# Attention into a channel mix: the first part's values in one PSUM tile, and a new order of all tasks

## The chip, the cores and the metric

The kernel runs on one core of one Trainium2 chip. The metric is the device time of one execution in microseconds, taken as the median of several. The profiles are single executions of the same program, recorded by the hardware profiler.

## The reference

Two stages for 8 batches of 576 positions. The first is attention in 8 heads of 64 channels with a mask that is causal by blocks of 64; the second takes its output as 512 channels and mixes them.

```python
scores = scale * np.matmul(q, k.transpose(0, 1, 3, 2))       # [8, 8, 576, 576]
scores = np.where(block_i >= block_j, scores, -1e9)          # blocks of 64
attn = np.exp(scores - max); attn = attn / (attn.sum(-1) + 1e-9)
x = np.matmul(attn, v)                                       # -> [8, 576, 512]
xk = mu_k * x + (1.0 - mu_k) * x_prev                        # x_prev: one position back
xr = mu_r * x + (1.0 - mu_r) * x_prev
k = np.maximum(xk @ w_k, 0.0)                                # 512 -> 1024
out = 1.0 / (1.0 + np.exp(-(xr @ w_r))) * (k * k @ w_v)      # 512 -> 512, 1024 -> 512
```

All inputs and the output are float32 in the chip's main memory.

## The kernel before

**Tasks.** The kernel is a list of 961 tasks, each for one engine: a load, a cast, a group of matmuls, an exponential and so on. They are written down in a fixed numbering. `ORDER` is a list of these numbers, written out by hand in the source, and gives the order in which they are issued; each engine works through its own tasks in that order. `PLACE` names for each flexible task (casts, squares, subtractions, copies out of PSUM) the engine that does it: P for GpSimd, D for VectorE, A for ScalarE. SyncE issues all transfers, also in the order of the list. A number with `+n` in `ORDER` puts n matmuls ahead of a TensorE task whose result nothing reads (`unread`, L253); they fill time in which TensorE would idle. A `B` task of the values does not issue its own, even where the list has a number for it.

**Buffers.** `RINGS` gives each kind of tile a number of buffers, and a task that needs a new one takes the one that was released first in the order of the list. PSUM has eight banks of 2 KB for each partition: three `s` tiles of two banks (`[128, 2, 512]` float32) and two `mm` tiles of one bank (`[128, 512]` float32). `s` tiles hold the transposed queries and keys, the scores, and the sums and values of the attention. `mm` tiles hold the products of the channel mix; at the start one of them is the target of the filling matmuls.

**A batch.** Queries and keys are loaded (`ld`), cast to bf16 (`nl`) and turned: in batches 0 to 2 by TensorE (`qt`, L312) with a copy out of PSUM (`ev`, L236 on ScalarE, L242 on VectorE), later by transposing transfers (`turn`, L357). Score tasks (`sc`, L458) write `s` tiles, ScalarE takes the exponential into `e` tiles (`ex`, L469). The values of attention are formed in two channel halves, A and B, by tasks `av`: A and B with the values (L517; L640 in batch 0), S with ones, which gives the sums (L507; L634). The sums are turned by VectorE (`t1`), inverted (`rec`), spread (`t2`), and `norm` multiplies them into the values and writes `x` (`xt`).

**Parts.** Batch 0 is done in two parts, positions 0 to 255 and 256 to 575, by `add_av_part` (`part` 0 and 1), so that the channel mix can begin early; the other batches are done in one by `add_av`. In the order A, S, B, the first task takes the even blocks of both halves and the last the odd ones. Task B starts with a scrap matmul into an unused corner of the sums' tile (L650), which makes TensorE wait until `t1` (L667) has read the sums.

**Before, each part takes three `s` tiles:**

```python
m = {kind: plan.buf("s") for kind in "SAB"}
```

one for the sums, of which one bank is used, and one for each channel half, with 256 or 320 columns in either bank. `norm` (L691) reads the half's tile and releases it.

**The channel mix.** For each batch and group of 128 channels there is a subtraction (`d`, L707) and a `mul` for `xk` and for `xr` (L729). Rows are then taken in chunks of 512 over the batches: `pk` multiplies with `WK` (L776), `relu` and `sq` give the squares in `k2` (L787, L789, L796, L798), `pr` multiplies with `WR` (L811), `tanh` follows (L821), `pv` multiplies with `WV` (L842), and `o` joins both (L854). `store` writes two tiles of 128 rows (L867). The weights are loaded as `ld` tiles and cast (`w`).

Of the kernel before, what the change touches and what calls it, by code (L numbers as in the profile page):

```python
# [14 lines left out]
LONGS = 3  # L15

ORDER = """
# [50 lines left out]
"""  # L68

PLACE = (  # L70
    "PPDPADPDPDDPPPAAPAAAADAADDDDDPPPPDPPPPDADDDPDDDPAPPPPDDAAPDDPAPAPA"
    "DDDPDDPDAAPDDDDAPAPDPPDDPAPAPDDPDPDPDDPPDPPDPAPDADDDAAPAADPDADPDDA"
    "PDAAPDDDADADAAADDAPAAAAAPAADPAAAPAADPDAAPAAADAPDPAPDAAADADAAPAPAPA"
    "AAAAADPAADAADADAAAPDPAAAAAPAPADAPADAPAPADAPAPAAAPADAPADDD")


class Plan:
# [53 lines left out]
def kernel(  # L131
# [12 lines left out]
    nc = tc.nc  # L144
    B, H, S, D = q.shape
# [44 lines left out]
    def new(buf):  # L190

        return slots[buf["ring"], buf["slot"]]
# [294 lines left out]

    HALVES = {"A": [*range(0, JT, 2)], "B": [*range(1, JT, 2)]}
    HALF = S // 2

    def blocks(b, PA, kind, ts=None):

# [120 lines left out]
    def add_av_part(b, part):  # L613
# [8 lines left out]
        exps = [ready["x", b, pr, i] for pr, i in its]  # L622
        vals = [cast["v", b, g] for g in range(2)] + [cast["vt"]]
        ebufs = [tiles["ebuf", b, it] for it in its]
        m = {kind: plan.buf("s") for kind in "SAB"}
        av = {}

        def products(f, t, at, n, i, col):
            for c in range(GH):
                E = new(tiles["ebuf", b, (c // 2, i)])  # L630
                out = slice(c * QC, (c + 1) * QC)
                flags = dict(start=t == 0, stop=t == pieces[-1][0])
                if f == "S":
                    nc.tensor.matmul(new(m[f])[out, 0, at:at + n],  # L634
                                     pick[:, (c ^ t) & 1],
                                     E[:, (c ^ t) & 1, col:col + n], **flags)
                    continue
                for u in range(2):
                    rows, w = weight(b, u, c, t, f)
                    nc.tensor.matmul(new(m[f])[out, u, at:at + n], w,  # L640
                                     E[rows, (c ^ t) & 1, col:col + n], **flags)

        tt, rc, rt = plan.buf("d"), plan.buf("rc"), plan.buf("rt")
        for kind in "ASB":
            def fn(eng, me, kind=kind):
                if kind != "B":
                    unread(me, new(m[kind])[:, 0])
                else:

                    nc.tensor.matmul(  # L650
                        new(m["S"])[0:QC, 0, CH - QC:CH], pick[:, 0],
                        new(ebufs[0])[:, 0, 0:QC], start=True, stop=True)
                for f in {"S": "S", "A": "AB", "B": "BA"}[kind]:
                    for t, lo, i, col, n in pieces:
                        if kind == "S" or t in HALVES[kind]:
                            products(f, t, lo, n, i, col)
            deps = exps + (vals if kind != "S" else [])
            if kind != "A":
                deps.append(t1m if kind == "B" else av["A"])
            av[kind] = add(  # L660
                f"av {b} {part} {kind}", "PE", fn, deps,
                uses=([m["S"]] if kind != "A" else [])
                + ([m["A"], m["B"], vo_buf[b]] if kind != "S" else [])
                + ebufs)
            if kind == "S":
                def t1(eng, me):
                    nc.vector.transpose(new(tt)[:, 0:W],  # L667
                                        new(m["S"])[:, 0, 0:W])
                t1m = add(f"t1 {b} {part}", "DVE", t1, [av["S"]],
                          uses=[tt, m["S"]])  # L670

        NB = W // QC

# [13 lines left out]
        for f in range(2):  # L687
            def norm(eng, me, f=f):
                x = new(xtbuf[b])[:, :, 1 + q_lo:1 + q_hi].rearrange(
                    "p (u f) t -> p u f t", f=2)  # L690
                nc.vector.tensor_tensor(  # L691
                    x[:, :, f], new(m["AB"[f]])[:, :, 0:W],
                    new(rt)[:, :, 0:W], ALU.mult)
            evac.setdefault(("x", b, part, f), []).append(
                add(f"norm {b} {part}{'AB'[f]}", "DVE", norm,
                    [av["B"]] + t2s, uses=[m["AB"[f]], rt, xtbuf[b]]))

    mixed = {}
    HC = CH // 2

    def add_mix(b, cc, part):
        d = plan.buf("d")
# [251 lines left out]
```

## Time and profile before

| | |
|---|---|
| median of 3 runs | 258.71 us (258.39 to 260.61) |
| the profiled execution | 258.73 us, its span 256.9 us |
| matmuls | 3425, TensorE busy 242.9 us |
| VectorE, ScalarE, GpSimd busy | 179.5, 172.8 and 83.8 us |
| mean granted TensorE clock | 0.992 |
| loaded and stored | 33.69 MB read, 9.44 MB written |

The span goes from the first to the last instruction on any engine. A busy share is taken over all of it. The granted clock is the share of full speed that TensorE was given. A row of the timeline has a start and a duration, the engine, the line of the kernel, the operation, the tile written and the tiles read, the shapes and the count; brackets behind it give the engine's idle time ahead of it and what ended that. A row of the groups has the busy time and the mean of one instruction in ns. "issue" as a releaser means that the engine waited for nothing that the profile shows.

### The profile page before, as it was taken

To read this page: it belongs to the slowest core of one execution; us is meant where nothing else is said; L and a number is where in the kernel's file an instruction comes from. 1 tells how busy PE (TensorE), PEld (TensorE's weight loads), DVE (VectorE), ACT (ScalarE), POOL (GpSimd) and SP (SyncE) were. 2 spreads that over 40 slices of the span, in tenths; PEclk is the share of its full clock that TensorE was granted. 3 is DMA by queue.
4 is the path that set the end of the run, shared out by engine and by line. 5 is a ranking of instruction groups with operands and counts; after the bars stand their busy time and mean duration, and the time that the engine had idled before them with its cause. 6 is when DMAs were issued, how large, how long until landed. Compare 5 with 4: busy or idle time off the path is not lost.

```text
span 256.9 us, 7885 instructions
## 1 busy us (share of the span) xinstructions
PE 242.9 (95%) x3425; PEld 121.8 (47%) x3425; DVE 179.5 (70%) x267; ACT 172.8 (67%) x234; POOL 83.8 (33%) x81
## 2 busy tenths in 40 slices
PE   7787779989999989999999999999999999999994
PEld 2454455745454435444544454445443554444452
DVE  1475969769879686997386978769868388622532
ACT  3597559989968866789688937974786851462330
POOL 2441356461334303302631026313613225170600
PEclk9999799999999999999999999999999999999999
DMA  7997999999999999999999999999961200400404
GB/s 215 393 282 172 391 287 243 348 258 176 270 207 160 261 206 199 233 229 232 198 192 268 185 171 208 276 234 214 194 149 74 92 3 0 164 4 0 165 3 163
DMA packets 119987, 49.54 MB, mean 193 GB/s; under 512 B 109584, under 2 KB 109840, under 8 KB 119952
## 3 DMA queue, kind: packets, MB, share of 16 engines
q1 hardware_dynamic: 119952, 49.04, 84.4%
q8 instruction: 27, 0.44, 0.8%
q14 instruction: 8, 0.07, 0.1%
HBM read 33.69 MB, written 9.44 MB: 168 GB/s over the span
## 4 chain that ended last, share of the span: by engine, by line
PE 79%; DVE 7%; DMA 5%; ACT 3%; issue 3%; SPq 2%; DVEq 0%; ACTq 0%
PE t_mm L776 24%; PE t_mm L842 21%; PE t_mm L811 11%; PE t_s L458 7%; PE t_s L517 7%; PE t_s L507 4%; DMA out_dram<-t_o 3%; SPq L225 2%; DMA t_ld<-in_q_dram 2%; DVE t_xk L729 2%; PE t_mm L253 2%; ACT t_e L469 1%; PE t_s L640 1%; ACT t_qkt L236 1%; DVE t_xt L691 1%
## 5 line engine op out<-in xcount | busy, mean ns | idle before, releaser
L469 ACT ACTIVATE t_e<-t_s 128x1024 f16<-128x1024 f32 (+3 forms) x98 | 87.8, 957 | 16.9 <-PE t_s L458 16.6
L776 PE MATMUL t_mm<-t_xk,WK 128*128 128x512 f16 (+1 forms) x320 | 69.7, 358 | 1.3 <-DVE t_xk L729 0.8
L842 PE MATMUL t_mm<-WV,t_k 128*128 128x512 f16 (+1 forms) x296 | 66.4, 374 | 0.3 <-DVE t_o L854 0.3
L798 POOL TENSOR_TENSOR t_k<-t_kr 128x512 f16<-128x512 f32 x30 | 34.0, 1141 | 73.2 <-ACT t_kr L787 43.0
L776 PEld LDWEIGHTS <-WK 128*128 128x128 f16 x320 | 29.3, 97 | 33.0 <-issue 7.6
L787 ACT ACTIVATE t_kr<-t_mm 128x512 f32<-128x512 f32 x48 | 28.7, 598 | 23.6 <-PE t_mm L776 23.5
L842 PEld LDWEIGHTS <-t_k 128*128 128x128 f16 x296 | 28.1, 98 | 33.8 <-issue 2.9
L854 DVE SCALAR_TENSOR_TENSOR t_o<-t_t,t_mm 128x512 f32<-128x512 f32 (+1 forms) x37 | 24.8, 670 | 24.6 <-PE t_mm L842 15.9
L811 PE MATMUL t_mm<-WR,t_xr 128*128 128x512 f16 x144 | 35.8, 380 | 0.0
L821 ACT ACTIVATE t_t<-t_mm 128x512 f32<-128x512 f32 x36 | 21.4, 597 | 16.8 <-PE t_mm L811 16.7
L458 PE MATMUL t_s<-t_qkt 64*64 64x64 bf16 (+7 forms) x680 | 29.1, 284 | 2.3 <-DVE t_xt L691 1.3
L729 DVE SCALAR_TENSOR_TENSOR t_xk<-t_d,MUK,t_xt 128x576 f16<-128x576 f32 (+4 forms) x44 | 29.7, 706 | 0.7 <-POOL t_d L707 0.6
L729 DVE SCALAR_TENSOR_TENSOR t_xr<-t_d,MUR,t_xt 128x576 f16<-128x576 f32 (+4 forms) x44 | 29.1, 671 | 1.1 <-POOL t_d L707 1.0
L707 POOL TENSOR_TENSOR t_d<-t_xt 128x576 f32<-128x576 f32 (+1 forms) x15 | 17.7, 1188 | 22.1 <-DVE t_xt L602 10.0
L458 PEld LDWEIGHTS <-t_qkt 64*64 64x64 bf16 x680 | 14.5, 106 | 20.4 <-issue 16.5
L242 POOL CAST t_nl<-t_ld 128x1152 bf16<-128x1152 f32 (+1 forms) x17 | 17.4, 1035 | 20.6 <-DMA t_ld<-in_k_dram 15.5
L789 DVE TENSOR_SCALAR t_kr<-t_mm 128x512 f32<-128x512 f32 x24 | 16.3, 684 | 8.7 <-PE t_mm L776 8.6
L796 ACT ACTIVATE t_k<-t_kr 128x512 f16<-128x512 f32 x29 | 17.9, 631 | 5.9 <-PE t_mm L842 5.3
L517 PE MATMUL t_s<-t_e,t_vo 64*32 64x64 f16 (+7 forms) x1106 | 20.6, 285 | 0.9 <-issue 0.9
L811 PEld LDWEIGHTS <-t_xr 128*128 128x128 f16 x144 | 12.9, 97 | 16.0 <-issue 2.5
L242 POOL CAST t_vo<-t_ld 128x1152 f16<-128x1152 f32 x9 | 10.2, 1145 | 31.4 <-DMA t_ld<-in_v_dram 31.4
L517 PEld LDWEIGHTS <-t_vo 64*32 64x32 f16 x1106 | 14.1, 92 | 10.4 <-issue 6.7
(51 smaller groups left out, 186.0 us busy)
## 6 DMA issues: line engine op xcount, KB each, us to landing
t_ld<-in_v_dram SPq DMA_DIRECT2D x32, 288.0 KB, 5.3
out_dram<-t_o SPq DMA_DIRECT2D x17, 512.0 KB, 4.1
t_ld<-in_q_dram SPq DMA_DIRECT2D x24, 288.0 KB, 5.3
t_ld<-in_k_dram SPq DMA_DIRECT2D x24, 288.0 KB, 5.2
t_ld<-in_k_dram SPq DMA_DIRECT2D x4, 576.0 KB, 7.8
t_ld<-in_q_dram SPq DMA_DIRECT2D x4, 576.0 KB, 8.1
t_ld<-in_moe_w_k_dram SPq DMA_DIRECT2D x4, 512.0 KB, 7.6
t_ld<-in_moe_w_v_dram SPq DMA_DIRECT2D x4, 512.0 KB, 6.6
```

Source lines behind the costliest of these rows:

```text
L242: e.tensor_copy(dst, src)
L458: nc.tensor.matmul(PS[y * D:y * D + D, x, col:col + n], operand(b, u, c, 1)[:, t * D:t * D + D], operand(b, u, c, 0)[:, q0:q0 + n], start= ...
L469: nc.scalar.activation(new(ebuf)[:, :, 0:w], new(m)[:, :, 0:w], AF.Exp, scale=ISQ)
L517: nc.tensor.matmul(PA[out, u, HALF + f * D:HALF + f * D + D] if kind == "T" else PA[out, u, lo - D:lo - D + n], w, E[rows, bank, at:at + n ...
L729: nc.vector.scalar_tensor_tensor(around[name][:, cc, at:at + w], new(d)[:, lo:lo + w], (MUK1, MUR1)[n][:, cc:cc + 1], x, ALU.mult, ALU.add)
L776: nc.tensor.matmul(ps[:, n], WK[:, cc, jc * P:(jc + 1) * P], xk[:, cc, lo:lo + w], start=(cc == 0), stop=(cc == CCn - 1))
L787: nc.scalar.activation(new(kr), new(m), AF.Relu)
L798: (nc.vector if eng == "DVE" else nc.gpsimd).tensor_tensor(dst, KR, KR, ALU.mult)
L811: nc.tensor.matmul(new(m), xr[:, cc, jt * P:(jt + 1) * P], WR[:, cc], start=(cc == 0), stop=(cc == CCn - 1))
L821: nc.scalar.activation(new(tb), new(m), AF.Tanh, scale=0.5)
L842: nc.tensor.matmul(new(m)[:, 0:w], k2[:, jc, jt * P:(jt + 1) * P], WV[:, jc, lo:lo + w], start=(jc == 0), stop=(jc == JCn - 1))
L854: nc.vector.scalar_tensor_tensor(new(o)[:, u, lo:lo + w], new(tiles["tbf", c, jt])[:, lo:lo + w], 1.0, new(m)[:, 0:w], ALU.add, ALU.mult)
```

## The change

`add_av_part` asks whether both halves of the part fit side by side: a part of up to 256 positions (`HC`) gets one `s` tile for A and B, B behind A in either bank, and its sums go to an `mm` tile. Only the first part of batch 0 is so short. Since A and B then share banks, only matmuls of A carry the start and stop flags. The second part, of 320 positions, keeps three `s` tiles. Besides, `ORDER` and `PLACE` are new throughout: all tasks are in another order, with other filling matmuls, and flexible tasks move between engines.

```diff
 ORDER = """
-11 12 15 0+12 17 18 13 14 16 51 52 49 50 73+3 3 74 127 128 7 5 125 75 9 6 79
-121 69+4 80 70 4 123 139+1 19 126 21 8 76 10 71 72 140 45 46 124 77+2 23 47
...
+11 12 17 0+12 13 14 49+1 15 16 18 50 7 8 51 9 10 3 5 125 52 121 47+4 6 71 48
+72 19 67 21 68 79+5 126 77 78 4 80 45+1 75 137 46 23 53+1 122 76 59 138 54
...
 PLACE = (
-    "PPDPADPDPDDPPPAAPAAAADAADDDDDPPPPDPPPPDADDDPDDDPAPPPPDDAAPDDPAPAPA"
...
+    "PPDDADDPDDDDAAAPAAADADDAADDPDDPPPPPDDDPDADADPPDDPPPPPDADAPDDDDPDPD"
...
 def add_av_part(b, part):
...
-        m = {kind: plan.buf("s") for kind in "SAB"}
+        one = W <= HC
+        ab = [plan.buf("s") for _ in range(1 if one else 2)]
+        sums = plan.buf("mm" if one else "s")
         av = {}
+
+        def dest(f):
+            if f == "S":
+                return new(sums) if one else new(sums)[:, 0]
+            n = "AB".index(f)
+            if one:
+                return new(ab[0])[:, :, n * W:(n + 1) * W]
+            return new(ab[n])[:, :, 0:W]
...
-                flags = dict(start=t == 0, stop=t == pieces[-1][0])
+                mine = f in "SA" or not one
+                flags = dict(start=mine and t == 0,
+                             stop=mine and t == pieces[-1][0])
...
-                    nc.tensor.matmul(new(m[f])[out, u, at:at + n], w,
+                    nc.tensor.matmul(dest(f)[out, u, at:at + n], w,
                                      E[rows, (c ^ t) & 1, col:col + n], **flags)
...
-                uses=([m["S"]] if kind != "A" else [])
-                + ([m["A"], m["B"], vo_buf[b]] if kind != "S" else [])
+                uses=([sums] if kind != "A" else [])
+                + (ab + [vo_buf[b]] if kind != "S" else [])
                 + ebufs)
...
-                    x[:, :, f], new(m["AB"[f]])[:, :, 0:W],
+                    x[:, :, f], dest("AB"[f]),
                     new(rt)[:, :, 0:W], ALU.mult)
...
-                    [av["B"]] + t2s, uses=[m["AB"[f]], rt, xtbuf[b]]))
+                    [av["B"]] + t2s, uses=[ab[0 if one else f], rt, xtbuf[b]]))
```

The order that the list gives each engine, seen in the built program ("the listing"): at the start the same four half loads stand first, in another sequence. The four half loads of the other heads' queries and keys of batch 0 come next, and the keys of those heads are turned ahead of the first score. In the first part's time two score tasks, one turn and their exponentials stand in the tiles that are left free. The filling matmuls that are issued are 42 instead of 35. By engine, VectorE has 3 `long` casts, 4 `v` casts, 2 `w` casts and 5 `sq` more and 2 `qk` casts, 1 `ev` and 1 `d` less; ScalarE has 5 `qk` casts and 1 `long` less and 1 `ev` and 1 `w` more; GpSimd has 7 `qk` and 1 `d` more and 2 `long`, 4 `v`, 3 `w` and 5 `sq` less.

More of the change, by code (lines that the diff above doesn't have):

```diff
@@ L17 @@
 ORDER = """
[50 rows of a table removed]
[50 rows of a table added]
 """
 PLACE = (
-    "PPDPADPDPDDPPPAAPAAAADAADDDDDPPPPDPPPPDADDDPDDDPAPPPPDDAAPDDPAPAPA"
-    "DDDPDDPDAAPDDDDAPAPDPPDDPAPAPDDPDPDPDDPPDPPDPAPDADDDAAPAADPDADPDDA"
-    "PDAAPDDDADADAAADDAPAAAAAPAADPAAAPAADPDAAPAAADAPDPAPDAAADADAAPAPAPA"
-    "AAAAADPAADAADADAAAPDPAAAAAPAPADAPADAPAPADAPAPAAAPADAPADDD")
+    "PPDDADDPDDDDAAAPAAADADDAADDPDDPPPPPDDDPDADADPPDDPPPPPDADAPDDDDPDPD"
+    "PPPDPAPPPAPDDPDAAPPDDPPDPDDPPPDPDDDDDPPPPDPDDAADADADPAPDDDPAPADDDD"
+    "ADPAADAAAAPAADPAAAAAAAADPDAAADPDADPDADAAAAADDAAAADDAPDPADAADAAAAAD"
+    "PADAAADAAAAADAPDPADAAAPDPADADADADAPAPADAPADADAPAPAPAPAPAD")
 class Plan:
@@ L489 @@
     HALF = S // 2
+    HC = CH // 2
     def blocks(b, PA, kind, ts=None):
@@ L631, in products @@
                 out = slice(c * QC, (c + 1) * QC)
-                flags = dict(start=t == 0, stop=t == pieces[-1][0])
+                mine = f in "SA" or not one
+                flags = dict(start=mine and t == 0,
+                             stop=mine and t == pieces[-1][0])
                 if f == "S":
-                    nc.tensor.matmul(new(m[f])[out, 0, at:at + n],
+                    nc.tensor.matmul(dest(f)[out, at:at + n],
                                      pick[:, (c ^ t) & 1],
@@ L646, in fn @@
                 if kind != "B":
-                    unread(me, new(m[kind])[:, 0])
+                    unread(me, new(ab[0])[:, 0] if kind == "A" else
+                           new(sums) if one else new(sums)[:, 0])
                 else:
                     nc.tensor.matmul(
-                        new(m["S"])[0:QC, 0, CH - QC:CH], pick[:, 0],
+                        dest("S")[0:QC, CH - QC:CH], pick[:, 0],
                         new(ebufs[0])[:, 0, 0:QC], start=True, stop=True)
@@ L667, in t1 @@
                     nc.vector.transpose(new(tt)[:, 0:W],
-                                        new(m["S"])[:, 0, 0:W])
+                                        dest("S")[:, 0:W])
                 t1m = add(f"t1 {b} {part}", "DVE", t1, [av["S"]],
-                          uses=[tt, m["S"]])
+                          uses=[tt, sums])
         NB = W // QC
@@ L695, in add_av_part @@
                 add(f"norm {b} {part}{'AB'[f]}", "DVE", norm,
-                    [av["B"]] + t2s, uses=[m["AB"[f]], rt, xtbuf[b]]))
+                    [av["B"]] + t2s, uses=[ab[0 if one else f], rt, xtbuf[b]]))
     mixed = {}
-    HC = CH // 2
     def add_mix(b, cc, part):
```

96 rows, old and new, of the table ORDER are left out of this document.

## The prediction

> **What bounds the kernel now.** I read the page first: busy shares, then the 40 slices.
>
> ```profile
> span 256.9 us, 7885 instructions
> PE 242.9 (95%) x3425; PEld 121.8 (47%) x3425; DVE 179.5 (70%) x267; ACT 172.8 (67%) x234; POOL 83.8 (33%) x81
> PE   7787779989999989999999999999999999999994
> PEclk9999799999999999999999999999999999999999
> ```
>
> TensorE is busy 95% of the span, and its digits fall below 9 in the first seven slices, some 45 us, and at the end. What a change can win is therefore mostly in those 45 us, while the queries, keys and weights still arrive. Next the busy times by stretch (columns: busy us and count of the engines, granted clock, DMA share, GB/s), first for all engines in long stretches, then for PE alone.
>
> ```profile
> 0.00:45.00 45.00, 36.74 (x651) 21.50 (x652) 28.83 (x52) 28.81 (x35) 17.85 (x25) 0.96 0.97 283
> 45.00:95.00 50.00, 48.34 (x790) 24.78 (x788) 40.37 (x59) 42.48 (x53) 17.75 (x15) 1.00 1.12 237
> 95.00:250.00 155.00, 154.29 (x1968) 73.73 (x1967) 108.43 (x155) 101.49 (x147) 48.24 (x42) 1.00 0.75 154
> ...
> 23.00:24.00 1.00, 0.39 (x36) 1.00 0.80 186
> 24.00:25.00 1.00, 0.37 (x17) 1.00 0.79 279
> 26.00:27.00 1.00, 0.21 (x4) 1.00 1.03 383
> 28.00:29.00 1.00, 1.00 (x6) 0.50 1.01 394
> 29.00:30.00 1.00, 1.00 (x18) 0.50 1.04 401
> 30.00:31.00 1.00, 1.00 (x64) 0.50 1.05 404
> ...
> 0.00:33.95 33.95, 27.71 (x478) 0.95 0.95 296
> 0.00:54.15 54.15, 45.88 (x862) 0.97 0.97 293
> ```
>
> PE idles 8.3 us up to 45, 1.7 from 45 to 95, 0.7 from 95 to 250. Inside the first stretch two things lie close together: PE is less than half busy around 23 to 27 us, and then its clock is halved for 3 us, which costs 1.5 us of matmul time. PE's timeline says what it waited for (start, us, instructions, then the idle time before and its releaser).
>
> ```profile
> 10.17 0.72 PE L458 MATMUL t_s<-t_qkt 64*64 64x320 bf16 x24 [0.56 <-ACT t_qkt L236]
> 22.38 0.89 PE L640 MATMUL t_s<-t_e,t_vo 64*32 64x256 f16 x32
> 23.87 0.46 PE L634 MATMUL t_s<-t_e,pick 128*32 128x256 f16 x16 [0.61 <-ACT t_qkt L236]
> 24.96 0.18 PE L650 MATMUL t_s<-t_e,pick 128*32 128x32 f16 x1 [0.63 <-DVE t_d L667]
> 26.79 0.28 PE L458 MATMUL t_s<-t_qkt 64*64 64x192 bf16 x4 [0.97 <-DVE t_xt L691]
> 27.39 0.90 PE L458 MATMUL t_s<-t_qkt 64*64 64x320 bf16 x12 [0.32 <-DVE t_xt L691]
> 32.53 1.05 PE L776 MATMUL t_mm<-t_xk,WK 128*128 128x256 f16 x8
> 35.86 1.12 PE L640 MATMUL t_s<-t_e,t_vo 64*32 64x320 f16 x78 [1.92 <-issue]
> 55.01 1.29 PE L517 MATMUL t_s<-t_e,t_vo 64*32 64x64 f16 x65 [0.86 <-issue]
> ...
> 91.33 1.89 PE L842 MATMUL t_mm<-WV,t_k 128*128 128x512 f16 x8 [0.30 <-DVE t_o L854]
> 94.13 0.38 PE L776 MATMUL t_mm<-t_xk,WK 128*128 128x512 f16 x1 [0.34 <-DVE t_o L854]
> 196.41 1.02 PE L776 MATMUL t_mm<-t_xk,WK 128*128 128x512 f16 x4 [0.53 <-DVE t_xk L729]
> ```
>
> The first part of batch 0 holds all three `s` tiles from 22.4 until VectorE's `norm`s (L691) end at 27.3. Scores find no tile, and PE waits 0.61, 0.63, 0.97 and 0.32 us: 2.5 us. The 1.92 and 0.86 us are of another kind: nothing in the data is late, the engine had no instruction. 478 and 862 matmuls precede them, exactly 3 x 128 apart, and each matmul is two instructions, so I read them as late blocks of 256 instructions.
>
> **The change part by part.** (1) The first part takes one `s` tile for both channel halves and one `mm` tile for its sums; two `s` tiles stay free for scores. Matmul and VectorE instructions of the part keep their count and shapes. (2) All tasks are in a new order. (3) Flexible tasks change engine. (4) Idle-filling matmuls (L253): those that are issued go from 35 to 42 by the listing. Prices:
>
> ```profile
> L469 ACT ACTIVATE t_e<-t_s 128x1024 f16<-128x1024 f32 x21 | 20.6, 1030 | 5.5 <-PE t_s L458 5.5
> L469 ACT ACTIVATE t_e<-t_s 128x256 f16<-128x256 f32 x2 | 0.8, 405 | 0.0
> L242 DVE COPY t_qkt<-t_s 128x1152 bf16<-128x1152 bf16 x7 | 9.4, 1350 | 3.5 <-PE t_s L312 3.5
> L236 ACT COPY t_qkt<-t_s 128x1152 bf16<-128x1152 bf16 x4 | 4.5, 1133 | 4.9 <-PE t_s L312 4.9
> L242 DVE CAST t_nl<-t_ld 128x576 bf16<-128x576 f32 x3 | 2.3, 753 | 6.3 <-DMA t_ld<-in_k_dram 5.2 <-DMA t_ld<-in_q_dram 1.0
> L729 DVE SCALAR_TENSOR_TENSOR t_xr<-t_d,MUR,t_xt 128x256 f16<-128x256 f32 x4 | 1.8, 451 | 0.0
> L798 DVE TENSOR_TENSOR t_k<-t_kr 128x512 f16<-128x512 f32 x1 | 0.7, 675 | 0.0
> ...
> 13.44 0.66 PE t_s L312 x9
> 20.47 0.76 PE t_mm L253 x3
> 29.68 1.85 PE t_s L640 x82
> 31.53 1.07 PE t_s L634 x44
> ...
> 24.46 0.45 DVE L667 STREAM_TRANSPOSE t_d<-t_s 128x256 f32<-128x256 f32 x1 [1.29 <-PE t_s L634]
> 26.05 1.29 DVE L691 TENSOR_TENSOR t_xt<-t_s,t_rt 128x512 f32<-128x512 f32 x2
> ```
>
> I follow the new order with these. The same four half loads stand first, so the first score is taken at 10.2, as now (bounds 9.8 and 10.6, one cast either way).
>
> To the first part's products the longest chain is: score 0.4, two exponentials 2.1, transposes 0.7, three copies out of PSUM on VectorE 4.1, transposes 0.7, score 0.2, two short exponentials 0.8, some 0.05 for each hand-over: 9.7. They start at 19.9, not 22.4. Then to the end of the `norm`s: products 0.9, sums 0.5, from L667 to the first `norm` 1.6 (24.46 to 26.05), one cast that now stands between 0.75, both `norm`s 1.3: 25.0 to 25.2, not 27.3. Meanwhile scores go on in the two free tiles, and no wait of the four above is left at its place.
>
> To the end of the second part's products: ScalarE has four exponentials after 19.9 (4.1), a copy (1.1), a short and a long exponential (1.5), 26.7; products 1.85, a score 0.4, its exponential 1.03, at 30.0. Here is a new wait: the second part's sums take the tile of that exponential, and PE idles 1.0 us. Sums 1.07, first `pk` 1.05, last products 1.4: 33.5. Before, they end at 35.86 + 1.12 = 36.98. VectorE's queue up to that `pk` (three subtractions and six `mul`s at about 0.45, one weight cast of 0.75, 4.8 us from 25.2) ends at 30.0, ahead of it. The weight loads that it needs are listed behind casts of the first 15 us, some 6 us sooner than now. The gain is 3.5; one score tile (0.3) that stands ahead of this point now stands behind it, so **3.2 us**. The added fills, 7 x 0.25 = 1.8 us, are inside these times: they stand in front of waits. From here to the first `pv` I find no wait of PE above 0.4 us.
>
> The halved clock goes with the gaps. The longest gap on this walk is the 1.0 us, and no 4 us of it are less than 70% busy. [...]
>
> Late instruction blocks: the one that cost 1.92 us now ends in the first `pk`, 4 us after the one before, as now, but with fewer loads outstanding. It can cost 0 to 1.9; the walk has 0, I take 0.4. The one of 0.86 has 0.6 us more work in front of it: I take 0.4 off (bounds 0 and 0.86).
>
> Past 45 us PE is full, and the order only adds or takes small waits. All that are left after 55 us are released by VectorE. On VectorE the listing has 3 `long`, 4 `v` and 2 `w` casts and 5 `sq` more, and 2 `qk` casts, 1 copy and 1 subtraction less: 7 x 0.75 + 5 x 0.675 - 1.35 - 0.75 = 6.5 us more. VectorE has 9.6 us free from 45 to 95 and 46 from 95 to 250, so most is covered; bounds 0 and 6.5, taken 0.3, near the single waits above. The tail (a half product, `o`, a store) is as before.
>
> Sum: 256.9 - 3.2 + 0.4 - 0.4 + 0.3 = 254.0 of span. The profiled execution took 258.73 for a span of 256.9 (1.83 around it), and agrees with the median of 258.71: **255.8 us**.
>
> **The rivals.** *VectorE takes the gain back, and more* (slower). Some 4.5 of its 6.5 us stand ahead of batch 3's products in the listing, where it is already 81% busy and where PE's waits at 91 and 94 us are its own. If PE comes 3 us sooner and VectorE later, `norm`, `mul` and `o` are late, and PE waits for `xk`, `s` and `mm` tiles. It decides from where that free time is used up by 9.6 us of queueing. At worst all of it shows: 258.7 - 3.2 + 6.5 = 262.0. For it: every late wait names VectorE. Against it: 30% of the span VectorE is free.
>
> *The gain is lost to fetches and gaps*: the 1.9 us block wait stays, and the 1.0 us gap with its neighbours halves the clock again (1.5 us): 255.8 + 1.5 + 1.5 = 258.8, no change. For it: DMA's share is about 1 throughout the start. Against: fewer loads pend.
>
> *All of it comes in*: no block is late, and the VectorE waits after 90 us (0.30, 0.34 and 0.53) go with the new order: 258.7 - 3.2 - 0.9 - 1.2 = 253.4.
>
> **How the numbers follow.** Forecast 0.50, with its own range 254.2 to 257.4; VectorE 0.25; fetches and gaps 0.15; all of it 0.10. One per cent (2.6 us) is about what a measurement of this kernel can tell from no change: below 256.1 lie all of the last case and 0.35 of the forecast, so faster 0.45; within 1% 0.15 and 0.15, 0.30; slower 0.25. The range goes from 253.3 to 262.0.
>
> **What would show it.** Right: the first L640 near 20 us, the first L691 near 24, the end of L640 near 33.5; the granted clock at full from 25 to 32; no PE wait for L691 ahead of the second part; PE full after 45 us. Wrong: an "issue" wait of 2 us again, a clock of 0.5 again, or PE waits for VectorE after 45 us that sum to over 2 us. The prediction fails if the products of batch 1 don't end some 3 us sooner than at 56.3 us (55.01 + 1.29).

## The result: from 258.8 to 256.8 us, 0.6 to 0.8% faster

| | before | after |
|---|---|---|
| median | 258.81 us (256.67 to 263.24, 17 runs) | 256.83 us (255.68 to 258.49, 17 runs) |
| the profiled execution, its span | 258.73, 256.9 us | 256.73, 254.9 us |
| ratio, 95% interval | | 0.9938 [0.9918, 0.9957] |

The ratio leaves out slow executions and the medians do not, so the gain is 0.6% by the one and 0.8% by the other. The forecast was 255.8, its own range 254.2 to 257.4. The gain has the predicted sign, but by the medians two thirds of its size: it is clear of the noise, and below the 1% that was taken as the mark. In the changed kernel the lines behind the first part are 15 or 16 higher: L640 is now L655, L634 is L649, L650 is L666, L691 is L707, L729 is L744, L776 is L791.

The page of the changed kernel:

```profile
span 254.9 us, 7890 instructions
PE 241.2 (95%) x3432; PEld 122.4 (48%) x3432; DVE 194.2 (76%) x277; ACT 168.6 (66%) x230; POOL 81.7 (32%) x75
PE   7898788998889999999999999999999999999994
PEclk9999999999999999999999999999999999999999
```

Its busy times by stretch, all engines:

```profile
0.00:45.00 45.00, 37.57 (x680) 22.61 (x681) 33.21 (x58) 32.42 (x38) 13.27 (x19) 1.00 0.98 300
45.00:95.00 50.00, 47.38 (x774) 24.74 (x772) 46.03 (x59) 36.38 (x49) 21.39 (x17) 1.00 1.04 226
95.00:250.00 155.00, 155.00 (x1974) 74.30 (x1973) 113.86 (x159) 99.79 (x146) 47.05 (x40) 1.00 0.76 154
```

The clock is full throughout, with no trace of the 0.5 around 29 us. In the first 45 us PE is busy 0.8 us more, and at full clock it gets through 680 matmuls instead of 651. From 45 to 95 it is busy 1.0 us less than before, and from 95 to 250 it has no wait left. VectorE is busy 14.7 us more. PE's timeline, with every wait of a half microsecond or more from 25 us on:

```profile
19.69 0.52 PE L655 MATMUL t_s<-t_e,t_vo 64*32 64x256 f16 x32
25.86 0.66 PE L312 MATMUL t_s<-identb,t_nl 128*128 128x128 bf16 x9 [0.66 <-DVE t_xt L707]
29.50 1.15 PE L649 MATMUL t_s<-t_e,pick 128*32 128x320 f16 x44 [1.19 <-ACT t_e L469]
30.58 1.05 PE L791 MATMUL t_mm<-t_xk,WK 128*128 128x256 f16 x8
33.10 0.18 PE L666 MATMUL t_s<-t_e,pick 128*32 128x32 f16 x1 [1.47 <-DVE t_rt L698]
33.20 1.14 PE L655 MATMUL t_s<-t_e,t_vo 64*32 64x320 f16 x80
44.32 0.41 PE L458 MATMUL t_s<-t_qkt 64*64 64x448 bf16 x8 [0.54 <-ACT t_e L469]
52.98 1.36 PE L518 MATMUL t_s<-t_e,t_vo 64*32 64x64 f16 x80
60.48 0.77 PE L458 MATMUL t_s<-t_qkt 64*64 64x256 bf16 x24 [0.66 <-DVE t_qkt L242]
64.76 1.89 PE L857 MATMUL t_mm<-WV,t_k 128*128 128x512 f16 x8 [0.90 <-DVE t_o L869]
75.69 1.02 PE L791 MATMUL t_mm<-t_xk,WK 128*128 128x512 f16 x4 [0.68 <-DVE t_kr L804]
```

The reader can set the gain against before at four places: the first part's products begin 2.7 us sooner (22.38 to 19.69), the second part's products end 2.6 sooner (36.98 to 33.20 + 1.14 = 34.34), batch 1's products end 2.0 sooner (56.30 to 52.98 + 1.36 = 54.34), and the span is 2.0 shorter. So all that remains at the end is there at 54 us already.

The 1.47 us at 33.10 bears the name of a VectorE transpose (L698), but that one ended at 32.70, and the reading of the sums (L683), for which L666 has to wait, at 31.27, ahead of the 31.62 at which PE fell idle. It is the block wait again, as the count of matmuls and the instruction queue's packet show. These are the windows that end where matmul 350 begins and where the wait begins, before and after (the count is behind the busy time; up to four matmuls begin within 0.02 us, so that it can stand a few above 350):

```profile
0.00:30.14 30.14, 23.91 (x351) 0.96 0.94 283
0.00:33.64 33.64, 27.41 (x478) 0.95 0.95 295
...
0.00:27.06 27.06, 23.07 (x354) 1.00 0.95 290
0.00:31.37 31.37, 26.20 (x478) 1.00 0.97 304
```

And this is the row of the instruction queue, q8, for the window 33.25 to 33.50 before and 30.50 to 30.75 after; from 30.25 to 33.25 before and 27.25 to 30.50 after the queue has no row, and only the data queue works:

```profile
q8 instruction: 1, 0.02, 25.9%
...
q8 instruction: 1, 0.02, 24.8%
```

One packet starts there. The page counts 27 of them, 0.44 MB in all, some 16 KB each; the 6864 matmuls and weight loads (3432 of either) make 254 to a packet. The place in the program where a block begins is called its border below. The first matmul of the block begins some 2.5 us later in both kernels (35.86 and 33.10). So the block is already on its way while the one before it runs, and it can come too late for it. That became the main question of the experiments.

### The profile page after: what moved, and what is told of

The parts are those of the page before. It is cut to its first block, busy times and chain, and to the rows that moved or that the text cites. A ratio compares the mean times of both kernels' runs of the same rounds, so it can differ in the third digit from the quotient of the medians.

```text
span 254.9 us, 7890 instructions
## 1 busy us (share of the span) xinstructions
PE 241.2 (95%) x3432; PEld 122.4 (48%) x3432; DVE 194.2 (76%) x277; ACT 168.6 (66%) x230; POOL 81.7 (32%) x75
## 4 chain that ended last, share of the span: by engine, by line
PE 75%; DVE 15%; DMA 4%; issue 2%; POOL 1%; SPq 0%; ACT 0%; DVEq 0%; ACTq 0%
PE t_mm L857 23%; PE t_mm L791 22%; PE t_mm L826 11%; PE t_s L458 7%; PE t_s L518 6%; DMA t_ld<-in_k_dram 4%; PE t_s L508 3%; DVE t_xk L744 2%; DVE t_qkt L242 2%; DVE t_xr L744 2%; DVE t_nl L242 2%; DVE t_kr L804 1%; PE t_mm L253 1%; PE t_s L312 1%; DVE t_xt L603 1%
## 5 line engine op out<-in xcount | busy, mean ns | idle before, releaser
L469 ACT ACTIVATE t_e<-t_s 128x1024 f16<-128x1024 f32 (+2 forms) x98 | 87.6, 957 | 20.8 <-PE t_s L458 20.3
L791 PE MATMUL t_mm<-t_xk,WK 128*128 128x512 f16 (+1 forms) x320 | 70.0, 358 | 0.7 <-DVE t_kr L804 0.7
L813 POOL TENSOR_TENSOR t_k<-t_kr 128x512 f16<-128x512 f32 x25 | 28.4, 1143 | 73.0 <-ACT t_kr L802 29.6
L857 PEld LDWEIGHTS <-t_k 128*128 128x128 f16 x296 | 28.2, 98 | 33.5 <-issue 2.7
L791 PEld LDWEIGHTS <-WK 128*128 128x128 f16 x320 | 29.0, 97 | 31.3 <-issue 4.9
L242 POOL CAST t_nl<-t_ld 128x1152 bf16<-128x1152 f32 (+1 forms) x22 | 26.8, 1226 | 35.7 <-DMA t_ld<-in_k_dram 13.6
L826 PE MATMUL t_mm<-WR,t_xr 128*128 128x512 f16 x144 | 36.1, 379 | 0.2 <-DVE t_xr L744 0.2
L744 DVE SCALAR_TENSOR_TENSOR t_xr<-t_d,MUR,t_xt 128x576 f16<-128x576 f32 (+4 forms) x44 | 33.6, 771 | 0.1
L744 DVE SCALAR_TENSOR_TENSOR t_xk<-t_d,MUK,t_xt 128x576 f16<-128x576 f32 (+4 forms) x44 | 31.8, 744 | 1.8 <-POOL t_d L722 1.8
L722 POOL TENSOR_TENSOR t_d<-t_xt 128x576 f32<-128x576 f32 (+2 forms) x16 | 18.7, 1177 | 32.3 <-DVE t_xk L744 11.5
L804 DVE TENSOR_SCALAR t_kr<-t_mm 128x512 f32<-128x512 f32 x24 | 16.4, 684 | 10.2 <-PE t_mm L791 10.1
L813 DVE TENSOR_TENSOR t_k<-t_kr 128x512 f16<-128x512 f32 x18 | 12.9, 725 | 8.4 <-ACT t_kr L802 8.3
```

Of the source, the lines that this page charges most:

```text
L242: e.tensor_copy(dst, src)
L469: nc.scalar.activation(new(ebuf)[:, :, 0:w], new(m)[:, :, 0:w], AF.Exp, scale=ISQ)
L744: nc.vector.scalar_tensor_tensor(around[name][:, cc, at:at + w], new(d)[:, lo:lo + w], (MUK1, MUR1)[n][:, cc:cc + 1], x, ALU.mult, ALU.add)
L791: nc.tensor.matmul(ps[:, n], WK[:, cc, jc * P:(jc + 1) * P], xk[:, cc, lo:lo + w], start=(cc == 0), stop=(cc == CCn - 1))
L813: (nc.vector if eng == "DVE" else nc.gpsimd).tensor_tensor(dst, KR, KR, ALU.mult)
L826: nc.tensor.matmul(new(m), xr[:, cc, jt * P:(jt + 1) * P], WR[:, cc], start=(cc == 0), stop=(cc == CCn - 1))
```

## The experiments

The theory as predicted: the tiles and the order take away waits of the first part and with them the halved clock. The rival that grew out of the traces: the end of the second part is set by the block of instructions, and the waits ahead of it count only as far as they move the moment when that block is asked for.

**Each half of the change alone.** First the old order with the new tiles:

```diff
-<ORDER and PLACE of the changed kernel>
+<ORDER and PLACE of the kernel before>
```

> The order and the placement of before, with the new tiles of the first part (one s tile for both halves, sums in an mm tile). Theory A (the freed tiles give the gain at the start): PE no longer waits for the norms (0.97 and 0.32 us before), perhaps the clock stays up too; 256.9 to 257.6 us, the first part's norms as late as before (near 27 us). Theory B (the new order gives it, by what stands before the first part): no change, 258.4 to 259.0 us.

Measured: 259.19 us (257.92 to 259.91), ratio to before 1.0011 [0.9979, 1.0044]. Then the new order with the old tiles; for two tasks to find a tile, 74 and 58 had to move ahead of 81, and 61 to 64 behind 87:

```diff
-        one = W <= HC
+        one = False
```

> The new order with three s tiles in the first part; the two exponentials that hold s tiles (0 1 3 and 0 0 2) come ahead of its products, and two score tasks with their exponentials (0 4 and 0 5) behind its norms, since no tile is left for them. Theory A: PE waits for the norms again, 1.5 to 3 us in all between 20 and 27 us, the clock may halve; 258 to 260 us. Theory B: 256.5 to 257.2 us as with the new tiles.

Measured: 259.57 us (258.43 to 260.97), ratio 1.0022 [0.9987, 1.0057]. Neither half gains anything that is clear of the noise; together they gain 0.6%. PE's timelines of the two, old order first:

```profile
27.08 1.06 PE L458 MATMUL t_s<-t_qkt 64*64 64x320 bf16 x12 [1.51 <-DVE t_xt L707]
36.10 1.25 PE L655 MATMUL t_s<-t_e,t_vo 64*32 64x320 f16 x78 [2.61 <-issue]
...
22.69 0.18 PE L666 MATMUL t_s<-t_e,pick 128*32 128x32 f16 x1 [0.63 <-DVE t_d L683]
25.04 1.45 PE L458 MATMUL t_s<-t_qkt 64*64 64x320 bf16 x24 [0.56 <-DVE t_xt L707]
36.38 0.18 PE L666 MATMUL t_s<-t_e,pick 128*32 128x32 f16 x1 [1.32 <-DVE t_rt L698]
```

With the old order the free tile has nothing to fill it, and the scores wait 1.51 us for `norm` in one piece. With the old tiles the new order starts its first part early (19.9 us) and then meets the waits one after the other, the clock is at 0.5 from 23.0 to 29.8 us, and the lead is gone. In both the next block comes at 36.1 to 36.4, as before.

**The halved clock by itself.** The kernel before, with filling matmuls moved into its waits, their number kept:

```diff
-0+12 ... 101+3 ... 82 ... 65 ... 57
+0+8 ... 101 ... 82+2 ... 65+4 ... 57+1
```

> The kernel before, with its order and its tiles, but 7 of its filling matmuls are moved: 4 of the 12 at the start and 3 ahead of the second part go into the waits of 0.61, 0.97 and 0.32 us (2, 4 and 1 of them), so that the count of matmuls ahead of every block of instructions is the same. No work is left out. Theory F (the halved clock costs its 1.5 us by itself): the granted clock stays at 1.0 from 28 to 31 us, and the time falls to 257.2 to 257.7. Rival G (the block ahead of the second part's products comes no sooner, so that what the clock gives back is waited for there): the clock is full, but the wait of 1.92 us grows to 3 or more, the products still end at 36.5 to 37.0, and the time is 258.4 to 258.9. Rival H (7 fills of 0.25 us are too few): the clock still falls to 0.5, and the time stays.

Measured: 258.53 us (258.12 to 260.05), ratio 1.0006 [0.9977, 1.0035]. That is rival G's time, though its wait (3 us or more) was 2.62 and its end of the products (36.5 to 37.0) was 37.21. In the profiled execution the clock is full. PE waits for an exponential where its clock was halved before, reaches the block's border at 33.47 instead of 33.94, and waits there for longer:

```profile
28.00:29.00 1.00, 0.62 (x12) 1.00 0.96 331
29.00:30.00 1.00, 0.43 (x35) 1.00 1.06 410
30.00:31.00 1.00, 1.00 (x95) 1.00 1.04 401
...
29.57 0.71 PE L640 MATMUL t_s<-t_e,t_vo 64*32 64x320 f16 x47 [0.95 <-ACT t_e L469]
36.09 1.12 PE L640 MATMUL t_s<-t_e,t_vo 64*32 64x320 f16 x78 [2.62 <-issue]
```

So in the kernel before, the 1.5 us that the halved clock seemed to cost were hidden: without them matmul 350 begins only 0.25 us sooner (29.89 for 30.14) because of the wait of 0.95, the block wait is 2.62 instead of 1.92, and the products begin at 36.09 instead of 35.86. In 5 of the 12 executions the mean clock was 0.999 or 1.0, and their median is 258.25 us, still above the 257.2 to 257.7 of theory F. In the other seven it was 0.986 to 0.993, with a median of 259.42; where it fell there was not traced. The counterpart is the changed kernel without its fills:

```diff
-<every +n of ORDER but 0+12>
+
```

> The changed kernel without its filling matmuls, except for the twelve at the very start. If the fillings keep the clock up: a stretch at 0.5 between 10 and 33 us, 257.5 to 259 us. If they only stand in waits: clock at full and time within 0.4 us of the changed kernel. If they cost time: 255.5 to 256.3 us.

Measured: 258.05 us (256.01 to 260.42), ratio to before 0.9964 [0.9927, 1.0001], by the medians 1.2 us more than with the fills, though the two intervals overlap. Here the clock is at 0.5 from 20.7 to 31.0 us, and matmul 350 begins at 29.8 instead of 27.1. What the clock costs there is not separated: 1.7 of these 2.75 us are lost at 21.38, where PE waits 1.73 us for the cast of values (`t_vo`) whose load landed later than in the changed kernel, and most of that wait lies ahead of the clock's fall. The block comes in time for so late a PE, and no issue wait shows.

**The blocks by count.** 19 more matmuls at the start, in idle time, move every border 19 matmuls forward in the program:

```diff
     def first_spare(eng, me):
         spare["at"] = new(wbuf)
         unread(me, None)
+        for _ in range(20):
+            nc.tensor.matmul(new(wbuf)[:, 0:16], identb, identb[:, 0:16],
+                             start=True, stop=True)
```

> The changed kernel with twenty tiny matmuls (16 columns) in place of one of the twelve filling ones at the start: 19 matmuls more ahead of everything. Theory C (late block of 256 instructions): the gap of 1.47 us moves 19 matmuls forward, out of its place ahead of L666 and into the sums (L649, 44 matmuls), some 11 matmuls ahead of the first pk, with matmul count at the gap near 478 as before. Theory D (the wait is for VectorE's t_d or t_rt): the gap stays ahead of L666 at about 1.5 us.

Measured: 262.32 us, one run. The wait leaves L666 and cuts the sums in two, just where the count puts it:

```profile
29.63 1.04 PE L649 MATMUL t_s<-t_e,pick 128*32 128x320 f16 x33 [1.19 <-ACT t_e L469]
33.29 0.51 PE L649 MATMUL t_s<-t_e,pick 128*32 128x192 f16 x11 [2.62 <-issue]
```

So no datum is late there, and the VectorE name on the 1.47 us was wrong. The clock is halved from 31.3 to 38.1 us, inside this wait and behind it; that comes on top, and so does a later wait of 2.03 us for `t_o` at 144 us that the shift doesn't explain. Then the border was moved by 52, to the start of those sums, where PE waits for an exponential anyway:

```diff
-0+12
+0+4
...
+        for _ in range(60):
```

> The changed kernel with 52 more matmuls at the start (60 short ones of 16 columns that nothing reads, 8 filling ones less), where TensorE waits for the first loads; no work is left out. In the runs so far the block that begins at matmul 478 came 5.7 to 6.3 us after matmul 350 began, in eight kernels, and with a quarter of two weights loaded within 4.8. Theory P (a block is asked for when the one before it is entered, and takes about 6 us beside the loads of this stretch): the blocks now begin at what were matmuls 298, 426 and 554 of the changed kernel. 298 begins near 23.4 us, so that the block at 426, the first matmul of the second part's sums, comes at 29.4, together with the exponential that they wait for (29.50); no issue wait stands ahead of L666 then, which begins near 31.6. 554, some 76 matmuls into the second part's 80, is asked for at 29.5 and comes at 35.5, so that an issue wait of 2.5 to 3 us stands inside or just behind the L655 matmuls, and they end at 35.2 to 35.8 instead of 34.34. Time 257.5 to 258.5. Rival Q (a block comes when the loads listed ahead of it have landed, whenever it was asked for): the block at 426 is late until 32 to 33 us, the one at 554 is there, the products end near 34.9. Rival R (the count of matmuls has nothing to do with it): the wait stays ahead of L666 with 1.5 us, and the products end at 34.3.

Measured: 260.07 us (258.37 to 262.0), ratio to before 1.0047 [1.001, 1.0084]:

```profile
31.08 1.15 PE L649 MATMUL t_s<-t_e,pick 128*32 128x320 f16 x44 [1.19 <-ACT t_e L469]
33.14 0.19 PE L666 MATMUL t_s<-t_e,pick 128*32 128x32 f16 x1
33.26 1.09 PE L655 MATMUL t_s<-t_e,t_vo 64*32 64x320 f16 x75
34.54 0.24 PE L655 MATMUL t_s<-t_e,t_vo 64*32 64x128 f16 x5 [0.19 <-issue]
```

Of theory P the places hold: nothing is late ahead of L666, and the next block is late 75 matmuls into the second part's 80, one off. The size fails: 0.19 us, not 2.5 to 3, since that block came 4.6 us after the border before it was reached (29.9), not 6. Rivals Q and R fall: Q had no wait at 554, R kept it at L666. Reaching the sums took 1.6 us longer than in the changed kernel (31.08 against 29.50), through waits for casts and `norm` around 23 to 27 us. Most of that was made good where the block's wait had been: the second part's products end at 34.78 and batch 1's at 54.78, each 0.44 later than in the changed kernel. The other 1.2 us of the profiled execution (258.37, below the median) arise behind that, with waits of 0.56 at 139.58 and 0.33 at 158.12.

**The transfers.** A quarter of the columns of `w_k` and `w_r` is loaded, and the casts repeat it; the products with the rest are left out of the answer:

```diff
-src[g * 2 * P:g * 2 * P + 2 * P, cols].rearrange(
+src[g * 2 * P:g * 2 * P + 2 * P, cols.start:cols.start + P].rearrange(
```

> The changed kernel, but only a quarter of the columns of w_k and w_r is loaded, and the casts repeat them four times: 2.4 MB less in transfers near 20 to 33 us, all instructions as before. If the block is late because it stands behind these transfers: the gap ahead of the last products falls below 0.4 us and the second part ends near 33 us, some 1 to 1.5 us sooner. If its time doesn't depend on the transfers: the gap stays at 1.2 to 1.6 us.

Measured: 258.28 us, one run. The issue wait ahead of L666 is gone, and the products end at 33.95 us, 0.4 sooner than after the change although they were reached later (matmul 350 at 27.7 instead of 27.1). The time did not follow. A new wait of 0.37 us for `xk` at 40.62 had taken the lead back by the end of batch 1's products (54.42 for 54.34), and further new waits of 0.2 to 0.4 us, most of them for VectorE, came behind. Then fewer bytes, but all of the work, by a change of the loads' order:

```diff
-35 33 ... 189 ... 187 ... 131 ... 129
+131 129 ... 35 ... 33 ... 189 ... 187
```

> The changed kernel, but the loads of batch 1's values (288 KB each) are issued where the two loads of w_r (512 KB each) were, these stand where the second queries' and keys' loads of batch 2 were, and those go behind them; the casts of w_r and the first product with it stand some ten tasks later. No work is left out. Theory A (the block of instructions ahead of L666 is late because it lies behind the transfers that are outstanding then): with 0.45 MB less ahead of it, about 1.2 us at the 375 GB/s of that stretch, the wait of 1.47 us falls to 0.3 to 0.8, the second part's products end at 33.2 to 33.8 instead of 34.34, and the time goes to 255.8 to 256.5 if nothing else becomes late. Rival B (the block comes at a fixed time after the one before, whatever is loaded): the wait stays at 1.3 to 1.6, the products end near 34.3, and the time is 256.8 or, if the first product with w_r is now late, up to 258.

Measured: 261.42 us (259.18 to 264.51), ratio to before 1.0092 [1.006, 1.0124]. Both expectations fail: in the profiled execution the block is later. The data queue from 28 to 34 us, this kernel first, then the changed one:

```profile
q1 hardware_dynamic: 4662, 1.43, 113.7%
...
q1 hardware_dynamic: 1538, 2.29, 104.1%
...
34.37 0.18 PE L666 MATMUL t_s<-t_e,pick 128*32 128x32 f16 x1 [2.37 <-issue]
```

The values come in small packets: three times as many for fewer bytes, 0.3 KB each instead of 1.5, and the engines are no less busy with them (113.7% of the 16 engines' time for 104.1%). By this trace bytes were the wrong measure. It is one execution, of 264.51 us, 3 us over the median, with the clock at 0.5 from 35.5 to 38.9 and from 45.8 to 52.6 us; what stands behind 35 us in it doesn't speak for the others, so why the median rose is not shown.

The kernels that have the border at matmul 478, worked out from windows like those above and ordered by when matmul 350 begins. "Packet" is the quarter microsecond in which the third block's packet starts, the last columns are the first matmul of that block where it was waited for, and the end of the second part's products:

| kernel | 350 begins | packet | block's first matmul | products end |
|---|---|---|---|---|
| 19 matmuls more | 26.95 | 30.75 | 33.29 | 37.60 |
| after | 27.06 | 30.50 | 33.10 | 34.34 |
| casts on ScalarE (below) | 27.41 | 30.50 | 33.14 | 34.38 |
| values ahead of `w_r` | 27.43 | 31.50 | 34.37 | 35.61 |
| scores behind the second part | 27.56 | 31.25 | 33.75 | 34.80 |
| a quarter of the weights | 27.74 | 29.00 | not waited for | 33.95 |
| no fills | 29.81 | 32.25 | not waited for | 35.73 |
| fills in the old waits | 29.89 | 33.25 | 36.09 | 37.21 |
| old order, new tiles | 30.01 | 33.25 | 36.10 | 37.35 |
| before | 30.14 | 33.25 | 35.86 | 36.98 |
| new order, old tiles | 30.49 | 34.00 | 36.38 | 37.62 |

The packet starts 3.1 to 4.1 us after matmul 350 begins where the loads are whole and the fills are in, 2.4 without fills, and 1.3 with a quarter of the weights. From the packet's quarter to the block's first matmul it is 2.4 to 2.9 us in all nine kernels that waited for it, and from matmul 350 to there 5.7 to 6.9 us. In eight of these nine the wait at the border is shown here: 1.32 us (new order, old tiles) to 2.62 (19 matmuls more, fills in the old waits). In seven of the eight the packet's quarter begins 0.2 to 1.1 us before PE reaches the border, with 19 matmuls more 0.1 behind that.

Behind batch 1's products TensorE takes much the same time in most kernels, whichever the order: 196.6 to 197.7 us up to its last product in eight of the twelve traces. In the other four it takes 198.1 to 198.4 (the two shifts and the quarter of the weights) and 203.0 (casts on ScalarE). So in those eight, what is gained or lost up to there stays.

**One score task less ahead of the second part.**

```diff
-136 147 99 ... 26 148 28 ... 104+4
+136 99 ... 26 28 ... 104+4 147 148
```

> The changed kernel, with one score task of batch 1 (1 03) and its exponential moved from ahead of the second part's sums to behind its last products. The sums then don't wait for that exponential (1.19 us in the changed kernel). Theory C (the 1.47 us ahead of the last products is a block of instructions that arrives late, at a time set by the transfers): the gap at the block grows by what the other one loses, time within 0.4 us of the changed kernel (256.5 to 257.2). Theory D (two separate waits, the second for VectorE): the second stays at 1.5 us or less, 255.5 to 256.0 us.

Measured: 258.47 us (257.67 to 261.46), ratio to before 0.9996 [0.9951, 1.0041]. Neither theory has its time. The wait of 1.19 us goes, and others take its place: `pk` waits 1.22 for VectorE's `xk`, the block wait comes 8 matmuls later in the program with 1.58, and the score that was moved brings a wait of 1.13 behind it. Batch 1's products end at 56.33 instead of 54.34.

```profile
30.77 1.03 PE L791 MATMUL t_mm<-t_xk,WK 128*128 128x256 f16 x8 [1.22 <-DVE t_xk L744]
33.75 1.05 PE L655 MATMUL t_s<-t_e,t_vo 64*32 64x320 f16 x73 [1.58 <-issue]
36.28 0.41 PE L458 MATMUL t_s<-t_qkt 64*64 64x512 bf16 x4 [1.13 <-ACT t_e L469]
```

**VectorE's longer instructions.** 14 casts of queries and keys go from GpSimd to ScalarE (`qk` tasks from P to A in `PLACE`).

> The changed kernel with the 14 casts of queries and keys (batches 3 to 7) that GpSimd does placed on ScalarE, in the same order. Theory E (VectorE stands still while GpSimd works, so its busy time grew by 14.7 us and not by 6.5): VectorE's busy time falls from 194.2 to 186 to 189 us, and the waits after 55 us that name VectorE (0.66, 0.90, 0.68) get shorter; 255.5 to 256.8 us unless ScalarE comes late. Theory F (VectorE's instructions got longer for another reason): 193 to 195 us busy, time 256.5 to 258.

Measured: 262.77 us (261.36 to 264.4), ratio to before 1.0142 [1.0039, 1.0245]. VectorE is busy 190.3 us, between the two expectations (186 to 189, and 193 to 195). One form of VectorE's groups, before, after, and with the casts moved:

```profile
L729 DVE SCALAR_TENSOR_TENSOR t_xr<-t_d,MUR,t_xt 128x576 f16<-128x576 f32 x20 | 16.1, 811 | 1.1 <-POOL t_d L707 1.0
...
L744 DVE SCALAR_TENSOR_TENSOR t_xr<-t_d,MUR,t_xt 128x576 f16<-128x576 f32 x20 | 18.6, 935 | 0.0
...
L744 DVE SCALAR_TENSOR_TENSOR t_xr<-t_d,MUR,t_xt 128x576 f16<-128x576 f32 x20 | 17.8, 892 | 0.0
```

The 20 instructions are the same in all three, and their means mislead: before, all 20 took 0.81 to 0.82 us; after, 17 still took 0.78 to 0.81 and three took 1.60 to 1.70; with the casts moved two took 1.60 and 1.70. The same holds for VectorE's other forms. Each instruction that took over 0.25 us more than its like began beside a GpSimd instruction that was already running (once it began within 0.02 us of it) and ended behind it. Before and after the change that was 0.02 to 0.62 us behind, for the `mul`s by columns: 0.21 to 0.22 us for 192, 0.34 to 0.35 for 320, 0.41 for 384 and 0.61 for 576. There are 8 of them before, 18 after and 12 with the casts moved, and their excess sums to 5.8, 13.7 and 9.2 us. So in part theory E is right, as far as which instructions meet. But the casts made ScalarE the late one: behind 100 us PE's waits for it sum to 3.85 us (1.85 for `t_e` at 124.50, 0.85 for `t_kr` at 183.21), of the 6.2 us by which its last product ends later.

## Why the prediction was right, and where it was not

*Right.* The first part's start: 19.69 for 19.9. The second part's first products: 26.67 for 26.7. The new wait of 1.0 us at the second part's sums: 1.19. First `pk` at 31.1 by the walk (30.0 and the sums): 30.58. Little changes behind batch 1's products, and the late waits all name VectorE. No halved clock: 1.00 throughout, but partly by luck, since the reason failed: of the 4 us from 28.4 PE was busy 2.12, 53%, where the walk had none below 70%.

*Wrong by the prediction's own marks.* The time lies in the range, yet by its last line the prediction fails: batch 1's products end 2.0 us sooner, not some 3. PE waited once for `norm` ahead of the second part. Its waits for VectorE behind 45 us sum to 2.62 us, over the 2 that were to be a sign of being wrong; before they were 1.47.

*The step that failed: the block of instructions as an independent term.* The walk took the 1.92 us block as something between 0 and 1.9, put 0.4, and added it to a chain of data. Measured were 1.47; since the first `pk` began 0.5 sooner than the walk had it, and the last products took 0.2 less, they ended at 34.34 instead of 33.5 + 0.4 = 33.9. More than a size was missed here. By the table, the block set this point in the kernel before and after; so the gain of 2.6 us is that matmul 350 begins 3.1 us sooner (30.14 to 27.06), less some 0.3 that the packet and its wait take longer and 0.1 since the block begins three matmuls earlier in the program. The four waits of the first part can count since they lie ahead of matmul 350. The halved clock (27.6 to 31.0) lies partly ahead of it and counted next to nothing: with a full clock PE waited for an exponential ahead of matmul 350 and for the block behind it, as the fills in the old waits showed, so the 1.5 us that "fetches and gaps" put on it were no term.

*The other terms.* `norm`s: foreseen 25.0 to 25.2, measured 25.80, and PE did wait for them once, 0.66 us at 25.86. VectorE's short `mu` instruction stood ahead of them for 1.11 us; below. Second block: 0.4 taken off, 0.86 measured, no issue wait is left from 34 us on; but waits of 0.24, 0.54 and 0.19 (0.97 in all) came in, one above the 0.4 that the walk allowed. From the second part's products to batch 1's PE needed 19.3 us before and 20.0 after, where the terms had it 0.1 less: this 0.8 is more than the 0.4 missed at the second part's end. The work between is the same but for the four score matmuls that were foreseen (0.3). VectorE: 6.5 us more work foreseen, 14.7 measured, since the price per instruction was taken as fixed; the instructions that GpSimd held up account for 7.9 of it. Of the waits it causes, 0.3 were foreseen; behind 56 us they sum to 0.66 + 0.90 + 0.68 = 2.24 against 0.30 + 0.34 + 0.15 + 0.15 + 0.53 = 1.47 before, so 0.8. The three after the change stand behind such held instructions of VectorE, at 57.45, 60.94 and 72.01 us; that they would go without them was not tested.

*The sum by measured terms.* 2.6 sooner at the second part, 0.7 lost by the end of batch 1's products: 2.0. Behind that the two kernels run alike. The last products, before and after:

```profile
247.35 6.22 PE L842 MATMUL t_mm<-WV,t_k 128*128 128x512 f16 x32
...
244.81 6.43 PE L857 MATMUL t_mm<-WV,t_k 128*128 128x256 f16 x34
```

They end at 253.57 and 251.24: from batch 1's products on PE took 197.3 us and 196.9, with 0.8 more of waits and 1.2 less of all else, and the rest of the span behind them went from 3.3 to 3.7 us. So the 2.0 stay. The rival "VectorE takes it back" had the mechanism for a part of the loss and the wrong size: with 14.7 us more, not 6.5, VectorE cost PE 0.8 more of waits behind 56 us. "Fetches and gaps" was half there, 1.47 of 1.9, without the clock.

*What stays open.* When exactly a block is asked for: the packet's delay of 1.3 to 4.1 us behind matmul 350 changed with the loads (1.3 with a quarter of the weights, 4.1 with the values ahead of `w_r`), and bytes alone don't order it. Whether a block in time would gain anything at the end: with a quarter of the weights the products came sooner and the time did not fall; its later waits were seen and not traced to their causes. And why the 375 matmuls behind the second part took 0.7 us longer, beyond the score task and 0.1 of waits.

## What to carry to other kernels

Count the instructions before you explain a TensorE wait at a point where transfers are dense: a wait that sits at a fixed count may be the next block of instructions, whatever name stands beside it, and a shift by a few cheap matmuls shows it. Here such waits stood behind 478 and 862 matmuls before, 3 x 128 apart, and behind 606, 128 more than 478, with 52 matmuls added. Work saved between matmul 350 and the block's arrival was waited away here (with the fills in the old waits the border was reached 0.47 us sooner and the wait grew by 0.70), so save it ahead. Look at single instructions before you trust a mean: three held ones made a mean of 20 grow from 811 to 935 ns. And two edits can be worth nothing apart and something together: a free tile needs an order that fills it.

## What the runs showed of the hardware that was not expected

*Some of VectorE's instructions were held beside GpSimd.* The `mu` instruction works on 4 values a partition and took 155 ns before. Here are its row before, then VectorE and GpSimd of the changed kernel:

```profile
22.94 0.15 DVE L888 TENSOR_SCALAR MUK<-MUK 128x4 f32<-128x4 f32 x1
...
23.43 1.11 DVE L903 TENSOR_SCALAR MUK<-MUK 128x4 f32<-128x4 f32 x1
24.53 1.27 DVE L707 TENSOR_TENSOR t_xt<-t_s,t_rt 128x512 f32<-128x512 f32 x2
...
23.38 1.15 POOL L242 CAST t_nl<-t_ld 128x1152 bf16<-128x1152 f32 x1 [8.73 <-PE t_s L312]
...
57.45 1.70 DVE L744 SCALAR_TENSOR_TENSOR t_xr<-t_d,MUR,t_xt 128x576 f16<-128x576 f32 x1
55.76 2.78 POOL L722 TENSOR_TENSOR t_d<-t_xt 128x576 f32<-128x576 f32 x2 [2.92 <-DVE t_xt L603]
...
74.23 0.81 DVE L744 SCALAR_TENSOR_TENSOR t_xr<-t_d,MUR,t_xt 128x576 f16<-128x576 f32 x1
```

It ends at 24.54, just behind the cast that GpSimd began 0.05 us earlier (23.38 + 1.15 = 24.53). The `t_xr` at 57.45 ends 0.61 us after GpSimd's work (59.15 and 58.54), while the same instruction at 74.23, with GpSimd idle, takes 0.81. Before and after the change, every subtraction and every `mul` of VectorE that began while a running GpSimd instruction had over 0.2 us left (8 and 15 of them) was held like this and ended 0.21 to 0.61 us after it. Of the instructions that read PSUM (`norm`, `t1`, the copies of turned queries and keys, `t_kr` and `t_o`) 37 and 24 began so, and none took over 0.02 us more than its like. The cast of `WV`, 1.53 us at 49.33 with 0.98 left of GpSimd's instruction, has no like to compare it with. GpSimd's own work is 2.1 us less than before (81.7 for 83.8), and VectorE's held instructions are 18 for 8: what counted is when it falls.

*The clock survives more idling than the prediction allowed.* From 28 to 31 us of the changed kernel PE is busy 1.81 of 3 us, and the clock stays at 1.00:

```profile
28.00:31.00 3.00, 1.81 (x56) 1.46 (x56) 2.85 (x8) 2.58 (x3) 0.00 (x0) 1.00 1.05 406
```

Before, the clock is at 0.5 for 3.41 us, from 27.62 to 31.03. By windows of 2 us it is so for 3.4 us from 26.7 on (old order, new tiles), 6.8 from 23.0 (new order, old tiles) and 10.2 from 20.7 (no fills): once, twice and three times as long. In the 3.41 us just ahead of the fall PE was busy 1.50 us before, 44%; by the timelines it was 47% with 19 matmuls more, 50% with the old order and 52% with the old tiles. This gives no limit: with the score task moved PE was busy 1.57 of the 4 us from 32, 39%, at a clock of 1.00, and with the casts on ScalarE 1.56 of the 3.41 us up to 124.50, 46%, in an execution with a mean clock of 1.000.
